# Query turns on quarters of the array, one tile for two kinds of turns, bias copies on a third engine, and a new list of steps

## The chip, the core and the metric

The kernel runs on one core of one Trainium2 chip. The core has five engines with an instruction queue each: TensorE (PE, matrix products, with its weight loads shown as PEld), VectorE (DVE), ScalarE (ACT), GpSimd (POOL) and SyncE (SP), which here only issues DMAs. Each engine works off its own queue in order; semaphores hold an instruction back until what it needs is done. [...] The metric is the device time of one execution in microseconds (us), lower is better.

## What is computed

Eight batches of linear attention (8 heads, 576 positions, head size 64), whose result goes, as 4608 tokens of 512 numbers, through a gated layer with two 512x512 weights:

```python
q_s = exp(q - max(q, -1));  q_s = q_s / sum(q_s, -1)      # over the head's 64 numbers
k_s = exp(k - max(k, 2));   k_s = k_s / sum(k_s, 2)       # over the 576 positions
kv  = einsum('bhsd,bhse->bhde', k_s, v)
x   = einsum('bhsd,bhde->bhse', q_s, kv)                  # then to (b s, h e)
H   = maximum(x @ w_h, 0)
T   = 1 / (1 + exp(-(x @ w_t + b_t)))
out = T * H + (1 - T) * x
```

## The kernel before

**Tiles.** The tokens make 36 tiles of 128. A pair of batches gives nine: four of the first batch, four of the second, and one that is half of each. Tiles 0, 4 and 5 are worked in two halves of the columns, and the last one (35) has its gate in two pieces.

**Order.** All work is written as a list of 683 steps, `ORDER` (line 16), and issued in that order with the scheduler switched off. A step's name gives the function, the batch or tile, and a part; a letter behind a colon gives the engine where there is a choice (A is ACT, D is DVE, P is POOL). Since every engine runs its own queue in order, the list fixes each engine's sequence; between engines the tile framework puts in the semaphore waits, from which tile each instruction writes and reads.

**A batch.** `q`, `k`, `v` (lines 180 to 206) issue the loads on SP's queue, on which the stores `st` stand too. `ek` and `eq` take exponentials on ACT, `vc` casts v (POOL, ACT or DVE). `kv` (262) sums k times v over the positions on PE: for batches from 2 on, 72 products of 64x64 by 65 columns, in which the row half of the array, `hh`, and the column half, `w`, change from one to the next, so that each quarter of the array has one in turn. The two row halves write to two PSUM banks. `kr` and `kn` normalise the result on DVE.

**The turn of q.** `qt` (310) transposes exp(q) of a batch in three groups, the first two (g = 0, 1) with eight products of 128x128 each against an identity, the third with two. It writes a tile `qps` of one PSUM bank from the pool `ps_q`, which holds one such tile. `qc` (329) copies it to SBUF (`eq`) on ACT or DVE.

**A tile.** `xu` (348) multiplies q with kv on PE, `rs` and `x` (367, 372) divide by q's sum on DVE. `xt` (379) transposes x on PE into the first half of a PSUM bank of its own, `turned`, and `xe` (387) copies that to SBUF (`xT`) on DVE or ACT. `bw` (394) puts the bias into the gate's PSUM tile: a product with ones on PE, or, with A, a copy of the prepared rows `ball` on ACT. On top of it `mt` (406) adds four products with w_t, `mh` (414) makes four with w_h. `th` is the tanh on ACT, `dd` joins x and the product with w_h on DVE, `uu` multiplies the two (DVE, or, with P, two instructions on POOL), `oo` adds x on POOL, and `st` stores. `fill` (165) issues products of zeros on PE that nothing reads. Before the first `mh` the weight w_h, in two loads (`w_h_0`, `w_h_2`), has an identity subtracted on POOL (`whd`) and is cast on ACT (`whc`).

The lines that hold the turns' places (100, 101, 115; line 313 in `qt`, 381 in `xt`):

```python
ps_q = pool("ps_q", 1, space=PS)
ps_xt = pool("ps_xt", 1, space=PS)
turned = ps_xt.tile([P, 2, 4, P], FP16, tag="xtps", name="turned")
t = T[f"qps{b}_{g}"] = ps_q.tile([P, a, 4, s * NP], FP16, tag="qps", name=f"qps_{b}_{g}")
t = T[f"xtps{i}"] = turned[:, 0]
```

Of the kernel before, what the change touches and what calls it, by code (L numbers as in the profile page):

```python
# [8 lines left out]
FP32 = mybir.dt.float32  # L9
# [12 lines left out]
wtc_2:P whc_2:A mh_1_0 wtc_0:P vc_1_3 ek_1_3 ek_1_2 vc_1_0 xe_3_0:D mh_3_0 dd_1 xt_0_1 xt_0_0 mt_1_0 xe_0_0:D mh_0_0
xe_0_1 dd_3 xt_2_0 mh_0_1 mt_0_1 th_1_0 xe_2_0:D dd_0 vc_1_2:A kv_1_1 uu_1_0 oo_1_0 eq_1_0 mt_0_0 th_0_0 ek_1_0 ek_1_1
kr_1_1 bw_3 qt_1_0 vc_1_1:A kn_1_1 qc_1_0 mt_3_0 xu_5_1 uu_0_0 mh_2_0 th_3_0 bw_2 rs_5_1 x_5_1 dd_2 xu_4_1 kv_1_0
kr_1_0 eq_1_1 rs_4_1 xt_5_1 mt_2_0 th_2_0 kn_1_0 bw_5 xe_5_1:D x_4_1 xu_5_0 mt_5_1 qt_1_1 eq_1_2 rs_5_0 x_5_0 xt_5_0
xu_4_0 bw_4:A uu_3_0:P oo_3_0 xe_5_0:D mh_5_1 rs_4_0 x_4_0 mh_5_0 xt_4_1 qc_1_1:A xt_4_0 xe_4_1:D dd_5 eq_2_0 xe_4_0:D
v_4_0 mt_5_0 th_5_0 xu_6_0 qt_1_2 rs_6_0 qc_1_2 oo_0_0 mt_4_1 mh_4_1 mh_4_0 uu_2_0:P x_6_0 mt_4_0 eq_2_1 xt_6_0 xu_8_0
uu_5_0 bw_6:A xe_6_0:D qt_2_0 rs_8_0 x_8_0 mh_6_0 oo_5_0 th_4_0 xt_8_0 dd_4 uu_4_0 xu_7_0 mt_6_0 ek_2_0:F rs_7_0
vc_2_2:A bw_8 xe_8_0:D mt_8_0 x_7_0 th_6_0 xt_7_0 th_8_0 oo_2_0 vc_2_0 kv_2_0 oo_4_0 qc_2_0 q_4_0 bw_7:A qt_2_1
qc_2_1:A dd_6 uu_6_0:P oo_6_0 eq_3_0:F xe_7_0:D kr_2_0 kn_2_0 mh_8_0 xu_9_0 rs_9_0 x_9_0 mt_7_0 th_7_0 bw_9 dd_8  # L30
uu_8_0:P qt_2_2 qc_2_2:A xu_10_0 bw_10:A xt_9_0 xe_9_0:D rs_10_0 x_10_0 ek_3_0 mh_7_0 dd_7 ek_3_2 mh_9_0 xu_12_0 k_4_0
xt_10_0 k_5_0 rs_12_0 qt_3_0 xe_10_0:D x_12_0 mt_9_0 th_9_0 uu_7_0:P q_4_9 dd_9 xu_11_0 qc_3_0 vc_3_2:A xt_12_0
mt_10_0 rs_11_0 mh_10_0 x_11_0 v_5_0 q_5_0 vc_3_0 st_1_1 q_5_9 uu_9_0 dd_10 oo_7_0 kv_3_0 qt_3_1 th_10_0 oo_8_0 st_1_0
xe_12_0 bw_12:A mh_12_0 kr_3_0 qc_3_1:A kn_3_0 xu_14_0 rs_14_0 x_14_0 bw_11:A xt_11_0 xe_11_0 mt_12_0 th_12_0 qt_3_2
v_6_0 xt_14_0 oo_9_0 k_6_0 xu_13_0 q_6_0 xe_14_0 mh_11_0 dd_12 qc_3_2 mt_11_0 rs_13_0 eq_4_0:F th_11_0 uu_12_0
uu_10_0:P x_13_0 dd_11 xu_15_0 rs_15_0 vc_4_0 mh_14_0 x_15_0 st_5_1 dd_14 qt_4_0 oo_10_0 vc_4_2 xu_16_0 rs_16_0 x_16_0
xt_13_0 xe_13_0:D oo_12_0 bw_14:A bw_13:A ek_4_0:F st_3_0 mt_14_0 th_14_0 xu_17_0 rs_17_0 bw_15:A x_17_0 qc_4_0
xt_15_0 mt_13_0 kv_4_0 xe_15_0:D kr_4_0 uu_11_0:P oo_11_0 th_13_0 qt_4_1 uu_14_0:P st_3_1 mh_13_0 vc_5_2 xt_16_0
kn_4_0 mh_15_0 xe_16_0:D vc_5_0 xu_18_0 ek_5_0:F dd_13 xt_17_0 qc_4_1:A uu_13_0 xe_17_0:D dd_15 rs_18_0 oo_14_0
bw_16:A mt_15_0 mh_16_0 x_18_0 th_15_0 uu_15_0:P mt_16_0 dd_16 mh_17_0 oo_13_0 bw_17:A th_16_0 oo_15_0 kv_5_0 uu_16_0  # L40
kr_5_0 kn_5_0 oo_16_0 eq_4_2 dd_17 qt_4_2 xt_18_0 eq_5_0 mt_17_0 st_5_0 xe_18_0 xu_20_0 rs_20_0 mh_18_0 qc_4_2:A
bw_18:A q_7_0 th_17_0 mt_18_0 eq_5_1 bw_20:A uu_17_0:P x_20_0 xt_20_0 dd_18 vc_6_2 xe_20_0:D xu_21_0 th_18_0 rs_21_0
st_7_0 v_7_0 qt_5_1 qc_5_1:A mt_20_0 x_21_0 xt_21_0 uu_18_0 eq_5_2 xu_19_0 xe_21_0:D qt_5_0 rs_19_0 x_19_0 st_7_1
mh_20_0 qc_5_0 bw_21:A st_10_1 vc_6_0 mt_21_0 th_20_0 dd_20 ek_6_0:F xu_22_0 bw_19:A rs_22_0 x_22_0 qt_5_2 th_21_0
qc_5_2:A eq_6_0 mh_21_0 bw_22:A xt_19_0 xe_19_0:D kv_6_0 dd_21 kr_6_0 kn_6_0 xt_22_0 uu_20_0:P mh_19_0 mt_19_0
xe_22_0:D dd_19 oo_17_0 xu_23_0 rs_23_0 oo_20_0 oo_18_0 mt_22_0 eq_6_1 qt_6_0 th_19_0 x_23_0 xu_24_0 uu_19_0 th_22_0
# [487 lines left out]
```

## Time and profile before

| | |
|---|---|
| time of three runs | 119.0, 119.03, 119.74 us; median 119.03 |
| span of the profiled execution, first to last instruction | 116.9 us |
| mean granted clock of PE | 0.995 of full |
| bytes moved by DMA | 40.58 MB, 347 GB/s over the span |
| instructions | 3424 |

The span is of one execution taken by the hardware profiler; a run's time also holds what lies before the first and behind the last instruction. The times of the runs are taken without the profiler.

How to read the rows that follow. A row of the timeline has the start in us, the time until the last of the group's instructions ended, the engine, the source line, the operation, the tile written and the tile read, the shape, and how many instructions of the kind stand in a row; a bracket behind it tells how long the engine had been idle and what ended that. PE overlaps its products: one of 128x512 is shown as some 0.38 us long though four of them start within 0.86, so PE's progress is read from start to start. A row of the windows view has the stretch and its length, then for each engine its busy time and its number of instructions, the granted clock, the DMA engines' share and GB/s. A row of the groups view has busy time, mean ns of one, and the idle time before them.

### The profile page before, as it was taken

The numbers are of one execution on the slowest core, as the hardware profiler recorded it, in microseconds if no ns is written. First come the engines' busy times: TensorE is split into PE (matmuls) and PEld (weight loads), VectorE is DVE, ScalarE is ACT, GpSimd is POOL, SyncE is SP. The second block draws the span as 40 slices with busy tenths as digits, with TensorE's granted clock in tenths as the row PEclk, the third lists the DMA queues.
The fourth block names the chain that finished last, engine by engine and source line by source line (L and its number), as shares of the span: only waits on it lengthen the run. The fifth ranks groups of instructions, "written<-read, shape, count | busy, mean of one in ns | idle before, by whom it ended". The sixth has DMA issues, their size and how long they took to land.

```text
span 116.9 us, 3424 instructions
## 1 busy us (share of the span) xinstructions
PE 109.5 (94%) x1351; PEld 61.6 (53%) x1351; DVE 93.3 (80%) x222; ACT 90.0 (77%) x132; POOL 89.1 (76%) x99
## 2 busy tenths in 40 slices
PE   5999987999999999999999999999999999999930
PEld 2354544545665656565665547566564555554520
DVE  5642587589799979979889798988989887899870
ACT  4356461897999999989999999998597998545520
POOL 5022237208996999999999999999989699999960
PEclk9999999999999999999999999999999999999998
DMA  2999999999999999999999999999999956992875
GB/s 42 399 392 377 408 398 385 375 377 379 393 391 397 383 391 393 358 375 387 357 376 360 387 392 363 390 381 383 399 398 217 302 204 270 397 404 115 315 295 179
DMA packets 24195, 40.58 MB, mean 347 GB/s; under 512 B 5362, under 2 KB 11762, under 8 KB 24180
## 3 DMA queue, kind: packets, MB, share of 16 engines
q1 hardware_dynamic: 24032, 40.24, 96.9%
q8 instruction: 10, 0.16, 0.6%
q10 hardware_dynamic: 148, 0.14, 0.4%
q14 instruction: 5, 0.04, 0.1%
HBM read 30.41 MB, written 9.44 MB: 341 GB/s over the span
## 4 chain that ended last, share of the span: by engine, by line
PE 67%; POOL 15%; issue 6%; DVE 5%; DMA 3%; SPq 1%; POOLq 0%; DVEq 0%
PE tps L411 18%; PE gps L419 16%; PE turned L167 9%; POOL o L471 7%; PE xu L361 6%; PE turned L384 5%; PE kv L269 5%; PE qps L324 4%; POOL u L451 4%; DMA out_dram<-o 3%; POOL g L450 2%; PE qps L319 2%; POOL v L259 2%; DVE x L376 2%; PE tps L401 1%
## 5 line engine op out<-in xcount | busy, mean ns | idle before, releaser
L471 POOL TENSOR_TENSOR o<-u,x 128x512 f32<-128x512 f16 (+1 forms) x36 | 40.6, 1143 | 1.6 <-DVE u L453 0.7
L411 PE MATMUL tps<-w16t,xT 128*128 128x512 f16 (+1 forms) x148 | 37.3, 373 | 0.0
L419 PE MATMUL gps<-w16h,xT 128*128 128x512 f16 x144 | 36.8, 379 | 0.5 <-DVE xT L391 0.5
L376 DVE TENSOR_TENSOR x<-xu,rs 128x512 f16<-128x512 f32 (+1 forms) x39 | 25.2, 649 | 2.4
L259 POOL CAST v<-v 128x1152 f16<-128x1152 f32 (+1 forms) x14 | 14.0, 1010 | 14.7 <-DMA v<-in_v_dram 13.7
L439 DVE SCALAR_TENSOR_TENSOR d<-x,gps 128x512 f16<-128x512 f16 x36 | 24.5, 680 | 0.3
L451 POOL TENSOR_TENSOR u<-g,d 128x512 f16<-128x512 f16 x17 | 19.7, 1158 | 1.7 <-DVE rs L370 0.4
L253 ACT ACTIVATE ek<-k 128x576 f16<-128x576 f32 (+2 forms) x15 | 17.9, 1225 | 3.0 <-DMA k<-in_k_dram 3.0
L419 PEld LDWEIGHTS <-xT 128*128 128x128 f16 x144 | 13.0, 98 | 12.3 <-DVE xT L391 1.8
L399 ACT COPY tps<-ball 128x512 f32<-128x512 f32 x28 | 16.6, 597 | 3.5 <-DVE u L453 3.2
L411 PEld LDWEIGHTS <-xT 128*128 128x128 f16 x148 | 13.2, 98 | 10.6 <-DVE xT L391 0.4
L361 PE MATMUL xu<-kvb,eq 128*128 128x130 f16 (+1 forms) x160 | 14.8, 224 | 0.2 <-DVE kvb L287 0.2
L384 PE MATMUL turned<-idh,x 128*128 128x128 f16 x144 | 14.2, 220 | 0.5 <-DVE x L376 0.5
L391 DVE COPY xT<-turned 128x512 f16<-128x512 f16 (+1 forms) x28 | 10.9, 391 | 4.2 <-PE turned L384 3.0
L435 ACT ACTIVATE tps<-tps 128x512 f32<-128x512 f32 (+1 forms) x20 | 11.2, 559 | 3.6 <-PE tps L411 3.3
L453 DVE SCALAR_TENSOR_TENSOR u<-tps,d 128x512 f16<-128x512 f32 (+1 forms) x19 | 12.7, 671 | 1.4 <-ACT tps L435 0.6
L361 PEld LDWEIGHTS <-eq 128*128 128x128 f16 (+1 forms) x160 | 10.0, 100 | 7.3 <-DVE x L376 2.5
L167 PE MATMUL turned<-blank 128*128 128x512 f16 x40 | 12.4, 458 | 1.5 <-POOL blank L149 1.3
L384 PEld LDWEIGHTS <-x 128*128 128x128 f16 x144 | 9.8, 98 | 6.0 <-DVE x L376 2.1
L307 ACT ACTIVATE qe<-q 128x1024 f16<-128x1024 f32 (+3 forms) x9 | 9.4, 1052 | 4.1 <-DMA q<-in_q_dram 4.1
L450 POOL TENSOR_SCALAR g<-th 128x512 f16<-128x512 f16 x17 | 10.6, 621 | 0.9 <-ACT th L433 0.9
L433 ACT ACTIVATE th<-tps 128x512 f16<-128x512 f32 x17 | 10.0, 594 | 0.9 <-PE tps L411 0.9
(48 smaller groups left out, 106.8 us busy)
## 6 DMA issues: line engine op xcount, KB each, us to landing
k<-in_k_dram SPq DMA_DIRECT2D x6, 1152.0 KB, 12.2
v<-in_v_dram SPq DMA_DIRECT2D x6, 1152.0 KB, 12.0
out_dram<-o SPq DMA_DIRECT2D x23, 256.0 KB, 4.0
q<-in_q_dram SPq DMA_DIRECT2D x10, 512.0 KB, 11.5
out_dram<-o SPq DMA_DIRECT2D x6, 512.0 KB, 3.8
k<-in_k_dram SPq DMA_DIRECT2D x4, 576.0 KB, 9.3
q<-in_q_dram SPq DMA_DIRECT2D x2, 1152.0 KB, 14.2
q<-in_q_dram SPq DMA_DIRECT2D x2, 640.0 KB, 10.5
```

Source lines behind the costliest of these rows:

```text
L167: nc.tensor.matmul(spare, blank[:, 0:P], blank, start=True, stop=True, skip_group_check=True)
L253: nc.scalar.activation(t[:, :, c:c + n].rearrange("p j c d -> p c j d"), T[f"k32{b}"][:, c:c + n].rearrange("p c (j d) -> p c j d", j=NJ), ...
L259: copy(v16[b % NV][:, c:c + n, :, 0:D], T[f"v32{b}"][:, c:c + n].rearrange("p c (j d) -> p c j d", j=NJ))
L361: nc.tensor.matmul(dst, turned_q(b, jp, n), kvb[b % NKV][:, hh, kk], start=True, stop=True, skip_group_check=True)
L376: nc.vector.tensor_mul(t[:, k0:k1], sums(i, k)[:, :, :, 0:64], T[f"rs{i}_{k}"][:, 0:k1 - k0].unsqueeze(3).to_broadcast([P, k1 - k0, 4, D]))
L384: nc.tensor.matmul(t[:, n], T[f"x{i}"][:, n0 + n % 2:n0 + 2 * P:2], idh, is_transpose=True, start=True, stop=True, skip_group_check=True)
L399: nc.scalar.copy(t[:, cs], ball[:, cs])
L411: nc.tensor.matmul(T[gate(i, k)][:, cs], T[f"xT{i}"][:, n], w16["t"][:, n, cs], start=False, stop=(n == parts[-1] and not first), skip_gro ...
L419: nc.tensor.matmul(t, T[f"xT{i}"][:, n], w16["h"][:, n], start=(first and n == parts[0]), stop=(n == parts[-1] and not (first and len(part ...
L439: nc.vector.scalar_tensor_tensor(t, T[f"x{i}"], -0.5, T[f"gps{i}"], op0=ALU.mult, op1=ALU.max)
L451: nc.gpsimd.tensor_mul(t, g, T[f"d{i}"])
L471: eng.tensor_add(t[:, cs], T[f"u{i}_{h}"][:, cs], T[f"x{i}"][:, cs])
```

## The change

Six things change.

1. The PSUM pools `ps_q` and `ps_xt`, one bank each, become one pool with one tile of two banks, `turned`, of which all turns of q and of x are slices.
2. For batches 2 to 6 and groups 0 and 1, `qt` issues, in place of eight transposes of 128x128, 32 of 64x64, in which the quarter of the array changes from one to the next; the upper row half writes to the first bank, the lower one to the second. `qc` puts the two together in its copy.
3. `xt` writes to the second bank, tiles of even number to its first half and of odd number to its second.
4. `bw` can copy the bias on DVE. Of 37 bias steps 9 were on PE and 28 on ACT; now 6 are on PE, 22 on ACT and 9 on DVE.
5. The other choices of engine: `uu` on POOL 17 to 20, `vc` on ACT 5 to 8 and on POOL 14 to 11, `xe` on ACT 11 to 16 and on DVE 28 to 23, `qc` on ACT 12 to 8 and on DVE 10 to 14.
6. The whole list is new (679 steps). It has 29 products of zeros instead of 40; the weights load in the order w_h_0, w_t_2, w_t_0, w_h_2 instead of w_h_0, w_h_2, w_t_2, w_t_0; on SP's queue nine stores stand ahead of k_7, as before, and ten instead of seven ahead of v_7.

The code, without the list:

```diff
-    ps_q = pool("ps_q", 1, space=PS)
-    ps_xt = pool("ps_xt", 1, space=PS)
+    ps_ab = pool("ps_ab", 1, space=PS)
...
-    turned = ps_xt.tile([P, 2, 4, P], FP16, tag="xtps", name="turned")
-    spare = turned.rearrange("p a c d -> p (a c d)").bitcast(FP32)
+    turned = ps_ab.tile([P, 2, 2 * DM], FP16, tag="ab", name="turned")
+    spare = turned[:, 1].bitcast(FP32)
...
+    QUADS = (2, 3, 4, 5, 6)
+
+    def corners(b, g):
+        return b in QUADS and g < 2
+
+    def qt_corners(b, g):
+        t = turned[:, :, g * DM:(g + 1) * DM]
+        for n in range(8):
+            for r in range(2):
+                rows = slice(64 * r, 64 * r + 64)
+                for c in range(2):
+                    cols = slice(64 * c, 64 * c + 64)
+                    if b in WIDE:
+                        main = T[f"qe{b}"].rearrange("p j c d -> p (j c d)")[:, 0:MAIN]
+                        main = main.rearrange("p (hh j kk f) -> p j hh kk f", j=4, hh=2, kk=2)
+                        src = main[rows, 2 * g + n // 4, n % 2, n % 4 // 2, cols]
+                        dst = t[cols, r, 64 * n:64 * n + 64]
+                    else:
...
+                    nc.tensor.matmul(dst, src, idh[rows, rows], is_transpose=True, start=True, stop=True,
+                                     skip_group_check=True)
+
     def qt(e, b, g):
+        if corners(b, g):
+            qt_corners(b, g)
+            return
...
-        t = T[f"qps{b}_{g}"] = ps_q.tile([P, a, 4, s * NP], FP16, tag="qps", name=f"qps_{b}_{g}")
+        t = T[f"qps{b}_{g}"] = turned[:, 0, 0:a * 4 * s * NP].rearrange("p (a n t) -> p a n t", a=a, n=4)
...
     def qc(e, b, g):
...
+        if corners(b, g):
+            src = turned[:, :, g * DM:(g + 1) * DM]
+            if b in WIDE:
+                copy(t.rearrange("p a n (r t) -> p r (a n) t", r=2), src.rearrange("p r (m t) -> p r m t", m=8))
+            else:
+                copy(t.rearrange("p a (k r) t -> p r (a k) t", r=2), src.rearrange("p r (m t) -> p r m t", m=4))
...
     def xt(e, i, k):
-        t = T[f"xtps{i}"] = turned[:, 0]
+        t = T[f"xtps{i}"] = turned[:, 1, i % 2 * DM:(i % 2 + 1) * DM].rearrange("p (n t) -> p n t", n=4)
...
     def bw(e, i, h=0):
...
         if e == "A":
             nc.scalar.copy(t[:, cs], ball[:, cs])
+        elif e == "D":
+            nc.vector.tensor_copy(t[:, cs], ball[:, cs])
```

(For the last tile's second gate piece `bw` uses the first bank of `turned` where it used `ps_q`.)

Places of the new list, in its own order, that the prediction speaks of:

```
... kv_1_0 qt_1_1 x_4_1 kr_1_0 kn_1_0 th_2_0 oo_1_0 uu_2_0:P xu_4_0 xt_4_1 rs_4_0 x_4_0 xu_5_0 rs_5_0 qc_1_1:A bw_4
xt_4_0 k_3_0 xu_7_0 oo_2_0 xe_4_1:D mh_4_1 mt_4_1 x_5_0 rs_7_0 th_3_0 eq_1_2 oo_0_0 x_7_0 xe_4_0 mt_4_0 bw_7:D xt_7_0
xe_7_0:D xu_6_0 eq_2_0 eq_2_1 q_3_0 uu_3_0:P qt_1_2 ...
... kv_3_0 qt_3_0 xt_11_0 uu_5_0:P oo_5_0 dd_12 qc_3_0:A bw_9:D mt_9_0 kr_3_0 kn_3_0 xe_11_0:D uu_12_0 qt_3_2 ...
... qt_4_0 uu_13_0:P q_5_9 x_15_0 bw_14:A qt_4_1 qc_4_0 kv_4_0 mh_16_0 dd_14 v_6_0 mt_14_0 eq_4_2 bw_16:A kr_4_0 kn_4_0
xu_18_0 oo_11_0 oo_13_0 qt_4_2 uu_9_0:P dd_16 qc_4_1:A xt_15_0 ...
... xt_20_0 xt_17_0 x_21_0 vc_5_0:A kv_5_0 dd_15 xe_17_0:D oo_14_0 kr_5_0 kn_5_0 dd_18 xe_20_0 qt_5_0 ...
... xt_23_0 oo_18_0 xe_23_0 eq_6_0 qt_5_2 mh_19_0 ...
... kv_6_0 qc_5_2 bw_24:D kr_6_0 q_7_9 qt_6_0 xt_25_0 xe_25_0 kn_6_0 dd_22 qc_6_0:A mt_24_0 xu_26_0 qt_6_1 ...
```

More of the change, by code (lines that the diff above doesn't have):

```diff
@@ L22 @@
[L22 to L46, printed above, removed]
@@ new lines @@
+dd_0 q_2_0 ek_1_2 mh_2_0 mt_2_0 dd_3 bw_3:A ek_1_1 dd_2 qc_1_0:A kv_1_1 mt_3_0 k_2_0 ek_1_0 vc_1_0 v_2_0 uu_0_0:P
+vc_1_1:D eq_1_1 kr_1_1 kn_1_1 xu_4_1 rs_4_1 qt_0_2 qc_0_2 kv_1_0 qt_1_1 x_4_1 kr_1_0 kn_1_0 th_2_0 oo_1_0 uu_2_0:P
+xu_4_0 xt_4_1 rs_4_0 x_4_0 xu_5_0 rs_5_0 qc_1_1:A bw_4 xt_4_0 k_3_0 xu_7_0 oo_2_0 xe_4_1:D mh_4_1 mt_4_1 x_5_0 rs_7_0
+th_3_0 eq_1_2 oo_0_0 x_7_0 xe_4_0 mt_4_0 bw_7:D xt_7_0 xe_7_0:D xu_6_0 eq_2_0 eq_2_1 q_3_0 uu_3_0:P qt_1_2 rs_6_0
+x_6_0 mh_4_0 dd_4 qc_1_2 mt_7_0 th_4_0 qt_2_1 xt_6_0 xe_6_0:D uu_4_0:P xu_8_0 rs_8_0 qc_2_1 ek_2_0:F x_8_0 bw_6:A
@@ new lines @@
+bw_16:A kr_4_0 kn_4_0 xu_18_0 oo_11_0 oo_13_0 qt_4_2 uu_9_0:P dd_16 qc_4_1:A xt_15_0 rs_18_0 qc_4_2 mt_16_0 eq_5_0
+eq_5_1 x_18_0 xu_17_0 xe_15_0:D th_14_0 bw_15:A rs_17_0 xt_18_0 qt_5_1 mt_15_0 oo_9_0 xe_18_0:D th_16_0 x_17_0 xu_20_0
+uu_16_0 oo_16_0 mh_18_0 uu_14_0:P rs_20_0 ek_5_0:F st_10_1 mh_15_0 bw_18:D x_20_0 xu_21_0 qc_5_1 st_10_0 rs_21_0
+mt_18_0 xt_20_0 vc_5_2:A xt_17_0 x_21_0 vc_5_0:A kv_5_0 dd_15 xe_17_0:D oo_14_0 kr_5_0 kn_5_0 dd_18 xe_20_0 qt_5_0
+mh_20_0 xt_21_0 dd_20 th_18_0 bw_17:A mt_17_0 th_15_0 uu_15_0 qc_5_0:A xe_21_0 xu_19_0 uu_18_0:P th_17_0 bw_20:A q_6_0
@@ L394, in bw @@
     def bw(e, i, h=0):
-        bank = (ps_t, "tps") if i < LAST or h == 0 else (ps_q, "qps")
-        t = T[gate(i, h)] = bank[0].tile([P, DM], FP32, tag=bank[1], name=f"tps_{i}_{h}")
+        if i < LAST or h == 0:
+            t = T[gate(i, h)] = ps_t.tile([P, DM], FP32, tag="tps", name=f"tps_{i}_{h}")
+        else:
+            t = T[gate(i, h)] = turned[:, 0].bitcast(FP32)
         cs = columns(i, h)
```

59 lines of the change are left out of this document (39 added, 20 removed).

## The prediction

> **What bounds the kernel now.** First the page's busy table, then the windows of ten microseconds, then PE's timeline and the chain of waits.
>
> ```profile
> PE 109.5 (94%) x1351; PEld 61.6 (53%) x1351; DVE 93.3 (80%) x222; ACT 90.0 (77%) x132; POOL 89.1 (76%) x99
> ```
>
> ```profile
> 60.00:70.00 10.00, 10.00 (x136) 5.44 (x134) 8.62 (x19) 9.34 (x14) 9.79 (x11) 1.00 1.07 378
> ```
>
> The columns after the window's length are busy PE, PEld, DVE, ACT, POOL, then granted clock, DMA share and GB/s. Four engines and the DMA are near full, but PE alone leaves nothing. A busy PE can hide waits, so I look at how closely its starts follow each other:
>
> ```profile
> 61.03 0.39 PE L384 MATMUL turned<-idh,x 128*128 128x128 f16 x4
> 61.25 1.03 PE L419 MATMUL gps<-w16h,xT 128*128 128x512 f16 x4
> 62.11 0.40 PE L361 MATMUL xu<-kvb,eq 128*128 128x130 f16 x4
> 62.35 0.39 PE L384 MATMUL turned<-idh,x 128*128 128x128 f16 x4
> 62.57 1.03 PE L411 MATMUL tps<-w16t,xT 128*128 128x512 f16 x4
> ```
>
> From start to start: four transposes of x (xt) 0.22 us, four products with w_h (mh) 0.86, four xu 0.24, and no hole. The stream runs so from about 20.8 us to its last group:
>
> ```profile
> 111.05 1.04 PE L411 MATMUL tps<-w16t,xT 128*128 128x256 f16 x8
> ```
>
> ```profile
> 113.07 0.41 DVE o L471
> ```
>
> The second line ends the chain of waits; behind it come only the last store and the end of the program. In the last third that chain runs over POOL, which works just behind PE's results. So the end is PE's stream plus a tail of some 5 us: what is added to the stream or put as a hole into it counts in full. The span is 116.9 us, the median of the runs 119.03, so 2.1 us lie outside the span; I add differences to 119.03.
>
> **The quarters.** Ten groups (two of each of batches 2 to 6) lose 8 transposes each and get 32 quarter transposes. No quarter transpose is in this trace; the nearest row is the key-value product kv, also on 64x64 quarters and issued in the same order of quarters.
>
> ```profile
> 9.87 0.48 PE L269 MATMUL kv<-v,ek 64*64 64x65 f16 x36
> 10.28 1.25 PE L167 MATMUL turned<-blank 128*128 128x512 f16 x5
> ...
> 41.98 0.38 PE L401 MATMUL tps<-b,ones 128*128 128x512 f16 x1
> 42.20 0.28 PE L324 MATMUL qps<-idh,qe 128*128 128x128 f16 x2
> ...
> 47.67 1.03 PE L419 MATMUL gps<-w16h,xT 128*128 128x512 f16 x4
> 48.62 0.78 PE L269 MATMUL kv<-v,ek 64*64 64x65 f16 x72
> 49.33 0.62 PE L324 MATMUL qps<-idh,qe 128*128 128x128 f16 x8
> 49.79 1.03 PE L419 MATMUL gps<-w16h,xT 128*128 128x512 f16 x4
> ...
> 57.38 0.42 PE L361 MATMUL xu<-kvb,eq 128*64 128x130 f16 x8
> 57.74 0.40 PE L384 MATMUL turned<-idh,x 128*128 128x128 f16 x4
> ```
>
> 36 products take 0.41 us, 72 take 0.71: 8.3 ns each and 0.11 fixed; and 48.62 is 0.09 later than four products after 47.67 would end, so a block on quarters standing alone pays 0.20. 32 quarters are 0.27 beside a kv and 0.47 alone, against 0.46 for the old eight. In the new list six groups touch a kv (2_0, 3_0, 4_0, 4_1, 5_0, 6_0), four stand alone: 6 x 0.19 saved, 4 x 0.01 lost, **-1.1 us**. The other end is the half-array xu at 57.38, 0.36 us for 8 of 130 columns, 22 ns for 64 columns: 32 of those are 0.71 us, +2.5 in all. I stay with kv, the same tile shape.
> [...]
>
> **Bias.** PE's own bias products (bw) go from nine to six at 0.22 (41.98 to 42.20): **-0.65 us**. DVE gets nine copies. None is in the trace; a bound above is 0.65 each, the DVE row that moves 512 f32 once, below it 0.42, DVE's xT copy of 512 f16:
>
> ```profile
> L376 DVE TENSOR_TENSOR x<-xu,rs 128x512 f16<-128x512 f32 (+1 forms) x39 | 25.2, 649 | 2.4
> ```
>
> ```profile
> 61.45 0.42 DVE L391 COPY xT<-turned 128x512 f16<-128x512 f16 x1 [0.53 <-PE turned L384]
> ```
>
> That is 3.8 to 5.9 us, less five xT copies that go to ACT (2.1) and three u at about 0.65 that go to POOL: DVE comes out 0.3 us below to 1.9 above its 93.3. No path by itself, but its cover gets thinner.
>
> **The start.** Fills fall from 40 to 29. They only fill waits for loads: nothing. But w_h_2 moves from the second to the fourth weight load.
>
> ```profile
> 15.13 0.89 POOL L226 TENSOR_TENSOR w32h<-w32h,idf 128x128 f32<-128x128 f32 x2 [0.38 <-DMA w32h<-in_moe_w_h_dram]
> 19.01 1.04 POOL L222 CAST w16t<-w32t 128x1024 f16<-128x1024 f32 x1 [0.27 <-DMA w32t<-in_moe_w_t_dram]
> ```
>
> ```profile
> 14.78 1.06 ACT L232 ACTIVATE w16h<-w32h 128x1024 f16<-128x1024 f32 x1 [0.90 <-POOL w32h L226]
> ```
>
> ```profile
> 18.14 1.03 PE L419 MATMUL gps<-w16h,xT 128*128 128x512 f16 x4
> 19.67 1.04 PE L419 MATMUL gps<-w16h,xT 128*128 128x512 f16 x4 [0.50 <-DVE xT L391]
> ...
> 20.76 1.03 PE L411 MATMUL tps<-w16t,xT 128*128 128x512 f16 x4
> ```
>
> The fourth load is there at 19.01 (the same eight loads stand ahead); its two subtractions take 0.89, its cast 1.06: PE gets the second half of w_h at about 20.96. Before, eight mh products and the transposes qt_0_2 were done by 20.76; now four mh: 0.86 + 0.11 of work left over, and 0.2 later: **+1.15 us**. If other waits cover it, 0.
>
> **The waits.** Before, x's transposes and q's transposes had tiles of their own. Now both are slices of one tile, `turned`, and in the changed kernel as built the waits go by the whole tile, halves and banks alike: qt_5_2, in the first bank, waits for the copy xe_23 out of the second. So places that the list treats as free are not. Prices of a hand-over:
>
> ```profile
> 30.52 0.29 DVE L391 COPY xT<-turned 128x256 f16<-128x256 f16 x1 [0.38 <-PE turned L384]
> ...
> 19.20 0.41 DVE L391 COPY xT<-turned 128x512 f16<-128x512 f16 x1
> ```
>
> ```profile
> 16.39 0.27 PE L324 MATMUL qps<-idh,qe 128*128 128x128 f16 x2
> ```
>
> ```profile
> 16.70 0.37 ACT L333 COPY eq<-qps 128x256 f16<-128x256 f16 x1 [0.86 <-PE qps L324]
> ...
> 49.99 1.01 ACT L333 COPY eq<-qps 128x1024 f16<-128x1024 f16 x1 [0.33 <-PE qps L324]
> ...
> 84.86 0.59 ACT L391 COPY xT<-turned 128x512 f16<-128x512 f16 x1 [1.45 <-PE turned L384]
> ...
> 99.41 0.60 ACT L391 COPY xT<-turned 128x512 f16<-128x512 f16 x1
> 99.88 0.62 ACT L399 COPY tps<-ball 128x512 f32<-128x512 f32 x1
> ```
>
> With the row at 61.45 above: a reader starts 0.42 after four transposes start (61.03, 61.45), 0.31 after two; an eq copy on ACT is 1.01, an xT copy 0.59 on ACT (the next on ACT starts 0.47 after it) and 0.42 on DVE, 0.29 for half; PE starts 0.06 after a copy ends (19.61, 19.67). In the new list, from PE step to PE step, less PE's own work between:
> xt_4_1, qc_1_1 on ACT, xt_4_0: 0.31+1.01+0.06, less 0.45: 0.93. Then xe_4_1, mh_4_1: 0.66 less 0.35: 0.31. xt_7, xe_7, qt_1_2: 0.90 less 0.46: 0.44. xt_11, qc_3_0 on ACT, xe_11 on DVE, qt_3_2: 1.97 less 1.08: 0.89. qt_4_2, qc_4_1 on ACT, xt_15: 1.38 less 0.11: 1.27. xt_17, xe_17, xe_20 on ACT, qt_5_0: 1.55 less 1.02 (kv_5 between): 0.53. xt_23, xe_23 on ACT, qt_5_2: 1.07 less 0.22: 0.85. xt_25, xe_25 and qc_6_0 on ACT, qt_6_1: 1.96 less 1.32: 0.64.
> PE runs in order, so behind each waiting transpose stand the next mh and mt, and for them th, dd and so POOL. Each stretch is separate, so the holes add: **+5.9 us**, more where ACT or DVE is late anyway. They are also pauses in which those engines catch up, so some of PE's small waits of before go. By the code 148 mt (eight of them of half size), 136 mh, 132 xt, 144 xu, 110 qt, eight blocks of kv and seven bw lie behind 20.76; at the spacings above they are 89.5 us of the 91.1 to the stream's end at 111.9. I take half of these 1.6 off, -0.8; bounds 0 and -1.6.
>
> Sum: -1.1 - 0.65 + 1.15 + 5.9 - 0.8 = +4.5: 123.5. As half of the start's term may be covered by other waits I take **123.0 us**.
>
> **Rivals.** (1) Waits by bank. If only accesses of the same bank excluded each other, the first three holes and qt_5_2 would vanish and qt_3_2 would keep 0.4: 3 us less, 120 us. [...] Against it stand the waits as built. It also holds the case that the holes are half as long. 0.10.
> (2) POOL sets the end, and the change is faster: the chain's last third lies on POOL.
>
> ```profile
> 26.56 0.67 POOL L259 CAST v<-v 128x576 f16<-128x576 f32 x1 [3.86 <-DMA v<-in_v_dram]
> ...
> 70.78 0.62 POOL L450 TENSOR_SCALAR g<-th 128x512 f16<-128x512 f16 x1
> 71.48 1.16 POOL L451 TENSOR_TENSOR u<-g,d 128x512 f16<-128x512 f16 x1
> 72.58 2.24 POOL L259 CAST v<-v 128x1152 f16<-128x1152 f32 x2
> ```
>
> Of its three added pairs of g and u (1.78 each) two, of tiles 0 and 1, come where POOL idled for loads, and three casts of v (1.12 each) leave it for ACT: 1.6 us less in the full stretch, 117.4. (ACT's sum so grows by some 1 us: five xT of 0.59 more too, six bias copies of 0.62 and four small eq of 0.37 less. The cast at 26.56 is POOL's last that waits for a load, so I cost it at nothing that v_7 stands behind ten stores on SP's queue instead of seven; k_7 has nine as before.) It decides if PE were several microseconds ahead of its readers, so that holes cost nothing; the gapless starts speak against it. 0.07.
> (3) Quarters at 22 ns: 3.6 us on top, 126.6. 0.05.
> (4) With fewer fills the clock drops in the start.
>
> ```profile
> 115.00:116.00 1.00, 0.00 (x0) 0.93 0.50 165
> ```
>
> PE stopped at 112 and the clock fell only near 115.9; the new start's longest pause, ahead of 20.96, is some 1.5 us by the loads' times. If it fell, up to 5.6 us (the first 13 fills at half speed) at half clock cost 2.8: 125.8. 0.04.
>
> **Numbers.** Forecast 0.74, its own range 121.0 to 125.3. One per cent, 1.2 us, is what a measurement of this kernel can tell from no change. Faster: rival 2 and a little of 1, 0.08. Same (117.8 to 120.2): most of 1, 0.09. Slower: the rest, 0.83. Range 120.3 to 125.5 leaves out rivals 2 and 3, part of 1 and of 4.
>
> **What would show it.** Right: PE holes of 0.5 to 1.3 us ahead of xt_15, qt_3_2, qt_5_2, qt_6_1 and near tile 4, released by copies of `turned`; quarters near 0.27 us beside kv; first mh of tile 1 whole only at 21 us. Wrong: PE starts as dense as before, or a chain without PE before 85 us.

## The result, and the profile after

The changed kernel takes **130.49 us** (median of five runs, 130.06 to 133.19) against 119.03 before: a ratio of **1.094, 95% interval 1.090 to 1.098**. It is slower, as forecast, but by 11.5 us where 4.0 were forecast, and 5 us above the range. The profiled run took 132.64 us at a lowered clock (a mean of 0.970 of full, against 0.98 in the undisturbed runs that the ratio rests on), so the times in its rows run up to 2 us late.

First the page of the changed kernel, busy time and two rows of the timeline in forty slices:

```profile
PE 110.7 (85%) x1577; PEld 62.0 (47%) x1577; DVE 94.9 (73%) x227; ACT 92.4 (71%) x130; POOL 90.6 (69%) x102
...
PE   5979667998689798979957688997998999999950
...
PEclk9999965899999999999999999999999999999998
```

PE was busy 94% before, now 85%, and every other engine has a smaller share too: the time is in waits, not in work. The timeline's end, PE's last group and DVE's last instruction, shows the same tail of some 5 us as before:

```profile
125.49 0.60 PE L448 MATMUL turned<-w16t,xT 128*128 128x256 f16 x4
```

```profile
127.05 0.42 DVE L508 TENSOR_TENSOR o<-turned,x 128x256 f32<-128x256 f32 x1
```

So the question is what delays PE's stream. The view of PE's waits adds them up by who ended them (total us, times, longest). All of before, 2.7 us:

```profile
PE turned L167 <- POOL blank L149: 1.3, 1, 1.3
PE gps L419 <- DVE xT L391: 0.5, 1, 0.5
PE turned L384 <- DVE x L376: 0.5, 1, 0.5
PE turned L167 <- DVE xT L391: 0.2, 1, 0.2
PE xu L361 <- DVE kvb L287: 0.2, 1, 0.2
```

After, the longest nine of 18 rows, which have 14.7 us in all (417 is `xt`, 349 a whole turn of q, 329 a quarter turn, 361 and 366 `qc`, 424 `xe`, 267 `kv`, 165 a product of zeros, 305 `eq`):

```profile
PE kv L267 <- issue: 2.7, 2, 1.8
PE turned L165 <- POOL blank L147: 1.3, 1, 1.3
PE turned L417 <- DVE eq L366: 1.3, 2, 1.0
PE turned L417 <- ACT eq L361: 1.1, 1, 1.1
PE turned L349 <- DVE xT L424: 1.0, 2, 0.7
PE turned L349 <- ACT qe L305: 0.8, 2, 0.5
PE turned L165 <- DVE eq L366: 0.8, 1, 0.8
PE turned L349 <- ACT xT L424: 0.8, 1, 0.8
PE turned L417 <- ACT eq L366: 0.8, 1, 0.8
```

Most rows are turns that wait for the copy of another turn out of the shared tile. The first is of another kind: `issue` means that PE waited for nothing the profile shows. The eight places that the prediction named are all there; here they are in the timeline, with the idle time in the bracket:

```profile
34.26 0.27 PE L417 MATMUL turned<-idh,x 128*128 128x128 f16 x2 [0.77 <-ACT eq L366]
...
34.99 0.60 PE L456 MATMUL gps<-w16h,xT 128*128 128x512 f16 x2 [0.22 <-DVE xT L424]
...
37.46 0.27 PE L349 MATMUL turned<-idh,qe 128*128 128x128 f16 x2 [0.35 <-DVE xT L424]
...
58.48 0.27 PE L349 MATMUL turned<-idh,qe 128*128 128x128 f16 x2 [0.70 <-DVE xT L424]
...
72.95 0.38 PE L417 MATMUL turned<-idh,x 128*128 128x128 f16 x4 [1.10 <-ACT eq L361]
...
81.82 0.45 PE L329 MATMUL turned<-idh,qe 64*64 64x64 f16 x32 [0.43 <-ACT xT L424]
...
89.70 0.27 PE L349 MATMUL turned<-idh,qe 128*128 128x128 f16 x2 [0.78 <-ACT xT L424]
...
98.96 0.45 PE L329 MATMUL turned<-idh,qe 64*64 64x64 f16 x32 [0.36 <-ACT eq L361]
```

The brackets sum to 4.7 us. A bracket counts from the end that the product before is shown with, which lies behind the moment at which the next could have started (the four transposes of x at 25.36 us are shown 0.39 long, and the next group starts 0.23 after them). From start to start, less the spacing of the product before (as the prediction reckons), the eight are 0.93, 0.39, 0.51, 0.86, 1.26, 0.64, 0.94 and 0.56 us, **6.1** in all, and the two without releaser 3.1.

By the brackets, with the 2.7 without releaser and the 2.7 that the kernel before had as well, 4.6 us of the 14.7 are left: 2.4 more than before in the first 22 us, and 2.2 strewn over the rest (more from start to start, as the part on the prediction works out). From 18 to 24 us the clock was at half speed too, which the prediction had given 0.04: columns as before, the sixth is the granted clock.

```profile
18.00:21.00 3.00, 2.33 (x16) 1.63 (x15) 1.09 (x3) 1.21 (x2) 2.59 (x5) 0.50 1.07 368
21.00:24.00 3.00, 3.00 (x13) 1.38 (x11) 1.16 (x3) 0.71 (x2) 0.08 (x1) 0.50 1.06 392
```

### The profile page after: what moved, and what is told of

Its sections match the earlier page's. It is cut to its first block, busy times and chain, and to the rows that moved or that the text cites. A ratio compares the mean times of both kernels' runs of the same rounds, so it can differ in the third digit from the quotient of the medians.

```text
span 130.9 us, 3893 instructions
## 1 busy us (share of the span) xinstructions
PE 110.7 (85%) x1577; PEld 62.0 (47%) x1577; DVE 94.9 (73%) x227; ACT 92.4 (71%) x130; POOL 90.6 (69%) x102
## 4 chain that ended last, share of the span: by engine, by line
PE 54%; DVE 22%; ACT 8%; issue 7%; DMA 4%; SPq 1%; POOL 0%; DVEq 0%; POOLq 0%
PE gps L456 15%; PE tps L448 14%; PE turned L165 7%; DVE x L409 7%; PE turned L417 5%; DMA out_dram<-o 4%; PE xu L394 4%; PE kv L267 4%; DVE d L476 3%; DVE u L490 2%; DVE xT L424 2%; ACT xT L424 2%; PE turned L329 2%; DVE eq L366 2%; DVE rs L403 2%
## 5 line engine op out<-in xcount | busy, mean ns | idle before, releaser
L488 POOL TENSOR_TENSOR u<-g,d 128x512 f16<-128x512 f16 x20 | 23.1, 1155 | 4.2 <-DVE d L476 1.8
L487 POOL TENSOR_SCALAR g<-th 128x512 f16<-128x512 f16 x20 | 12.3, 617 | 6.2 <-ACT th L470 6.2
L470 ACT ACTIVATE th<-tps 128x512 f16<-128x512 f32 x20 | 11.9, 596 | 6.6 <-PE tps L448 6.5
L434 ACT COPY tps<-ball 128x512 f32<-128x512 f32 x22 | 13.0, 593 | 1.4 <-DVE u L490 1.0
L424 DVE COPY xT<-turned 128x512 f16<-128x512 f16 (+1 forms) x23 | 9.2, 404 | 5.9 <-PE turned L417 3.5
L424 ACT COPY xT<-turned 128x512 f16<-128x512 f16 (+1 forms) x16 | 8.7, 546 | 6.7 <-PE turned L417 4.7
L257 POOL CAST v<-v 128x1152 f16<-128x1152 f32 (+1 forms) x11 | 10.5, 969 | 4.1 <-DMA v<-in_v_dram 4.1
L472 ACT ACTIVATE tps<-tps 128x512 f32<-128x512 f32 (+1 forms) x16 | 9.1, 568 | 5.3 <-PE tps L448 5.2
L403 DVE RECIPROCAL rs<-xu 128x8 f32<-128x8 f32 (+1 forms) x39 | 7.6, 198 | 5.4 <-PE xu L394 5.4
L490 DVE SCALAR_TENSOR_TENSOR u<-tps,d 128x512 f16<-128x512 f32 (+1 forms) x16 | 10.7, 668 | 0.9 <-ACT tps L472 0.4
```

Source lines behind the costliest of these rows:

```text
L424: copy(t[:, 2 * k0:2 * k1], T[f"xtps{i}"][:, 2 * k0:2 * k1])
L434: nc.scalar.copy(t[:, cs], ball[:, cs])
L488: nc.gpsimd.tensor_mul(t, g, T[f"d{i}"])
L490: nc.vector.scalar_tensor_tensor(t[:, cs], T[gate(i, h)][:, cs], 1.0, T[f"d{i}"][:, cs], op0=ALU.add, op1=ALU.mult)
```

## The experiments

The theories, by the numbers that the expectations use: (1) waits of the whole shared tile; (2) PE's instructions do not come fast enough where quarters and kv stand together; (3) the clock drops in the start; (4) the rest is the new list's own; (5) bias copies hold back VectorE. The rival of each is that its cost is hidden by something else. All times are medians; all ratios are to the kernel before, which ran beside each (118.89 to 119.03); a difference given "by the ratios" is that of two ratios, times 119 us.

| run | us | ratio, 95% interval |
|---|---|---|
| changed kernel | 130.49 | 1.094 (1.090 to 1.098) |
| split copies | 131.03 | 1.101 (1.097 to 1.105) |
| two tiles (and split copies) | 127.65 | 1.075 (1.072 to 1.077) |
| whole turns | 128.99 | 1.088 (1.082 to 1.094) |
| more fills | 131.51 | 1.107 (1.103 to 1.111) |
| other weight order | 131.07 | 1.100 (1.097 to 1.103) |
| bias on PE again | 132.54 | 1.114 (1.107 to 1.121) |
| three steps moved | 129.06 | 1.085 (1.077 to 1.093) |
| two tiles, whole turns | 125.05 | 1.052 (1.047 to 1.057) |
| the same, bias on PE again | 126.36 | 1.062 (1.059 to 1.065) |
| two tiles, quarters in three batches | 126.11 | 1.056 (1.051 to 1.062) |
| two tiles, whole turns, other weight order | 124.23 | 1.046 (1.040 to 1.051) |
| the same, four steps moved | 122.23 | 1.026 (1.021 to 1.031) |
| old list in the changed code | 134.73 | 1.132 (1.125 to 1.140) |
| before, one tile | 134.54 | 1.130 (1.125 to 1.135) |
| before, five bias copies on DVE | 121.59 | 1.021 (1.019 to 1.023) |
| before, more products | 126.85 | 1.065 (1.060 to 1.070) |

### The shared tile

Two tiles need the copy of a quarter group as two, so a control has that alone.

```diff
-            src = turned[:, :, g * DM:(g + 1) * DM]
+            for r in range(2):
+                src = turned[:, r, g * DM:(g + 1) * DM]
...
```

> The changed kernel, but the copy qc of each of the ten quarter groups is made as two, one per bank; the control for the run with two tiles. All theories: within 1 us of the changed kernel's 130.5 us (ten more copies; half of the copy of 1024 numbers costs little more than half). If PE's holes are set by how long these copies take, up to 2 us more.

```diff
-    turned = ps_ab.tile([P, 2, 2 * DM], FP16, tag="ab", name="turned")
+    turned = [ps_ab.tile([P, 2 * DM], FP16, tag=f"ab{r}", name=f"turned{r}") for r in range(2)]
```

> As the control with split copies, but the one tile of two banks is two tiles of a bank each, so that waits go by the bank. Theory 1 (the waits of the whole tile make the holes ahead of xt_4_0, mh_4_1, qt_1_2, qt_5_2, partly qt_3_2): 2 to 3 us less than the control, those holes under 0.2 us; the holes ahead of xt_15, qt_5_0, qt_6_1 stay, since quarters and copies lie in both banks. Rival (the holes are made good elsewhere, PE waits for its readers anyway): under 0.7 us less.

The control is 0.5 us over the changed kernel, the two tiles 3.4 under the control (3.1 by the ratios): theory 1, a little over the 2 to 3 that it gave. In PE's waits the copies ahead of xt_4_0, qt_1_2, qt_3_2 and qt_5_2 are gone, and the holes ahead of xt_15 (1.2 us), qt_5_0 (0.4) and qt_6_1 (0.3) have stayed, as expected. As the same turn then waits only for what lies in its bank, this is also what the first rival of the prediction would have been worth, had the waits gone by the bank.

The sharing alone, put into the kernel before:

```diff
-    ps_q = pool("ps_q", 1, space=PS)
-    ps_xt = pool("ps_xt", 1, space=PS)
+    ps_ab = pool("ps_ab", 1, space=PS)
...
+    QUADS = ()
...
+        t = T[f"xtps{i}"] = turned[:, 1, 0:DM].rearrange("p (n t) -> p n t", n=4)
```

> The kernel before with one edit: the turns of q and of x are slices of one tile (q in the first bank, x in the second, no quarters, its own list), so that each waits for the other's copies. Theory 1: clearly slower, by the waits of a list that was not made for it, 5 us or more (124 or more), with PE waiting for copies of the turns. Rival (waits by bank decide on the chip, the tile does not matter): within 0.5 us of 119.

It costs **15.5 us**, more than the whole change. The two longest of PE's waits in it, of 15.0 us in all where the kernel before had 2.7:

```profile
PE turned L418 <- DVE eq L367: 3.3, 3, 1.7
PE turned L418 <- ACT eq L367: 1.9, 4, 1.1
```

No work is added and no two places overlap; `xt` waits for copies of q's turns because they are slices of one tile. The old list with the quarters as well comes out the same (by the code, turns of x here overwrite parts of q's turn before these are copied, so what it computes is not the layer; no instruction is left out, and its time can be read):

> The changed kernel's code (one tile of two banks, quarters) with the list of the kernel before (bias on PE and ACT, its weight order, its fills). Theory 4 (most of what the two causes leave is the new list's own: its start, its order, its engines): below 126 us. Rival (the list was made for the shared places and the old one suffers more under them): 130 us or more.

134.73 us, the rival: the old list suffers more under the shared places than the new one, by 4.2 us. What the new list costs by itself shows only where the sharing is undone (below).

Do the holes count in full? Three steps of the changed kernel moved:

```diff
-... qt_1_2 rs_6_0 x_6_0 mh_4_0 ...
+... rs_6_0 x_6_0 mh_4_0 qt_1_2 ...
-... qt_5_2 mh_19_0 mt_19_0 ...
+... mh_19_0 mt_19_0 qt_5_2 ...
-... kv_4_0 ... qt_4_2 uu_9_0:P dd_16 qc_4_1:A xt_15_0 ...
+... kv_4_0 qc_4_1:A ... qt_4_2 uu_9_0:P dd_16 xt_15_0 ...
```

> The changed kernel with three steps moved in the list: qt_1_2 behind mh_4_0, qt_5_2 behind mt_19_0 (products that are ready hide the copy they wait for), and the copy qc_4_1 from behind qt_4_2 to behind kv_4 (so that xt_15 finds it done). Theory 1 (each hole is its own and counts in full to the end): 0.5 + 0.95 + 1.3 us by PE's starts, 2.3 to 2.8 less, about 127.9. Rival (the pauses let VectorE and ScalarE catch up, and what goes there comes back as another wait): under 1.2 us less.

1.4 us less (1.1 by the ratios, whose intervals overlap), nearer to the rival. The timeline says why. The hole ahead of qt_1_2 went, but the next turn then waited:

```profile
37.63 0.44 PE L329 MATMUL turned<-idh,qe 64*64 64x64 f16 x32 [0.57 <-DVE eq L366]
```

The hole ahead of xt_15 went for good. In the changed kernel ScalarE had stood idle there for 4.91 us, since its copy stood behind qt_4_2 in the list and so waited for that turn to be written to the same tile:

```profile
71.88 1.01 ACT L361 COPY eq<-turned 128x1024 f16<-128x1024 f16 x1 [4.91 <-PE turned L349]
```

### The quarters

```diff
     def qt(e, b, g):
-        if corners(b, g):
-            qt_corners(b, g)
-            return
...
+        if corners(b, g):
+            t = turned[:, :, g * DM:(g + 1) * DM].rearrange("p a (n t) -> p a n t", n=4)
```

> The changed kernel with the quarter turns undone: the ten groups are eight transposes of 128x128 each again, into the same places of the same tile, with the same list. My prediction's term: 1.1 us more than the changed kernel (131.6), since quarters beside kv are cheaper. Theory 2 (the unpaid term: after a dense stretch of quarters and kv PE runs out of instructions, the holes of 0.88 and 1.83 us inside kv_2 and kv_4 without any releaser): those two holes go, so 1.5 to 2 us less than the changed kernel (128.5 to 129). If the holes belong to kv alone they stay.

128.99, 1.5 us less: the quarters cost, where the prediction had them save 1.1. (By the ratios it is 0.7, and the intervals overlap; the same edit on two tiles, below, gains 2.6, clear of them.) Both holes without releaser are gone. In the changed kernel they stand inside kv_2 and kv_4, just behind quarter turns:

```profile
43.38 0.45 PE L329 MATMUL turned<-idh,qe 64*64 64x64 f16 x32
43.65 0.78 PE L267 MATMUL kv<-v,ek 64*64 64x65 f16 x70
45.30 0.22 PE L267 MATMUL kv<-v,ek 64*64 64x65 f16 x2 [0.88 <-issue]
...
66.17 0.70 PE L329 MATMUL turned<-idh,qe 64*64 64x64 f16 x64
66.86 0.64 PE L267 MATMUL kv<-v,ek 64*64 64x65 f16 x55
69.33 0.34 PE L267 MATMUL kv<-v,ek 64*64 64x65 f16 x17 [1.83 <-issue]
```

The kernel with eleven more fills ahead of them (below) has the same two holes, each eleven products earlier in its kv, after 59 instead of 70 and after 44 instead of 55:

```profile
41.88 0.69 PE L268 MATMUL kv<-v,ek 64*64 64x65 f16 x59
43.52 0.31 PE L268 MATMUL kv<-v,ek 64*64 64x65 f16 x13 [0.95 <-issue]
...
65.15 0.54 PE L268 MATMUL kv<-v,ek 64*64 64x65 f16 x44
67.02 0.42 PE L268 MATMUL kv<-v,ek 64*64 64x65 f16 x28 [1.32 <-issue]
```

So the hole belongs to a place in PE's instruction stream, not to a step. Counted in the program (a product and its weight load are two), it is instruction 959 and 1725 in both kernels, 766 apart. With PE's two semaphore instructions between them (at 55.00 and 66.75 us in the changed kernel) they are 768 apart, and of the packets that bring instructions there are three for this stretch (those that start at 49.38, 60.53 and 66.84 us): 256 a packet. The page counts the packets that bring instructions (queue, packets, MB), after and before:

```profile
q8 instruction: 12, 0.20, 0.6%
```

```profile
q8 instruction: 10, 0.16, 0.6%
```

That is 16 KB for some 256 of the 3156 and 2704 instructions. The trace also has the time of each of these packets, beside PE's holes (us; entered is PE's first instruction of the block before):

| hole | block before entered | packet moved | PE goes on |
|---|---|---|---|
| changed kernel, kv_2 | 39.95 | 42.88 to 43.98 | 45.30 |
| changed kernel, kv_4 | 64.70 | 66.84 to 68.07 | 69.33 |
| more fills, kv_2 | 37.62 | 41.00 to 42.05 | 43.52 |
| more fills, kv_4 | 61.10 | 64.52 to 65.72 | 67.02 |

In each, PE goes on 1.3 to 1.5 us after the packet with the next block has landed. Ten of the kernels here have such holes, 19 of 0.2 us and more: all stand at the same place of a block of 256, within one instruction, and all end 1.2 to 1.5 us after a packet. So in these rows the packet with the next block started 2.1 to 3.4 us after PE had entered the block before, and PE was through the two blocks of the changed kernel, with quarter turns and kv in them, at 44.24 and 67.30 us, 1.1 and 2.0 us too soon. The test away from the change is the kernel before with more small products in two places.

```diff
-            for j in range(NJ):
+            for j in ([0] * 16 if b in (3, 5) and kk == 0 else []) + list(range(NJ)):
```

> The kernel before with 64 more products on quarters in kv_3 and 64 in kv_5: the products of the first position block are made 16 times more in the same places, the last of them starting the sum anew, so that the result is the same. Theory 2: row 1983 of PE's instructions (blocks begin at rows 191, 447 and so on) falls near the end of kv_5, and the block before it is nothing but such products: a hole of 2.5 to 5 us without releaser just there, perhaps 1 us at row 1215 in kv_3; with the products' own 1.06 us the time is 122.5 to 126. Rival (instructions are no limit): 120.1, 8.3 ns for each product.

```profile
66.79 1.41 PE L269 MATMUL kv<-v,ek 64*64 64x65 f16 x132
72.41 0.27 PE L269 MATMUL kv<-v,ek 64*64 64x65 f16 x4 [4.21 <-issue]
```

One hole, within four instructions of the place foretold, 4.2 us long; its packet landed at 71.16 us. There is none in kv_3, where the block lasted 5.6 us. At 126.85 us the time is 0.85 over the range expected: of the 7.8 us lost, 1.06 are products and 4.2 the hole, and the rest is put down to the clock, at 0.82 in the ten microseconds behind.

In the changed kernel, does it help to use quarters only where they do not starve?

```diff
+        if b in (3, 5, 6) and g < 2:
+            qt_corners(b, g)
+            return
```

> Two tiles, and the quarters kept for batches 3, 5 and 6 alone; batches 2 and 4, beside whose kv PE ran dry, turn whole. Theory 2 (PE's instructions come in blocks of 256 rows, and a block that PE works off in less than some 5 us makes it wait): the holes without releaser inside kv_2 and kv_4 are gone, at most one of under 1 us at row 1215, and the quarters save their 0.19 us beside kv_3, kv_5 and kv_6: 124.4 to 125.3, at or under the 125.05 of whole turns. Rival (quarters cost by themselves, wherever they stand): 126 to 127.

Not clearly: the two holes went and the one of 0.75 us at instruction 1215 (at 53.52 us) is the one allowed for, but with 125.7 us by its ratio, between the two ranges, the kernel is 0.6 over two tiles with whole turns alone, the intervals overlapping. The quarters showed a saving in no run.

### The bias copies

```diff
-... bw_7:D ... bw_10:D ... bw_9:D ... bw_18:D ...
+... bw_7 ... bw_10 ... bw_9 ... bw_18 ...
```

> The changed kernel with the nine bias copies of VectorE made as products on PE again. My prediction's term (a copy on VectorE is free, a product on PE 0.22 us): 2.0 us more, 132.5. Theory 5 (as in the kernel before with five such copies: each holds VectorE 0.6 us, and x and the copies of x come late for PE): 0.5 to 2.5 us less, 128 to 130.

132.54: 2.05 more for nine, 0.23 each, near the prediction's 0.22. Theory 5 falls. It came from this run of the kernel before:

```diff
-... bw_3 ... bw_2 ... bw_5 ... bw_8 ... bw_9 ...
+... bw_3:D ... bw_2:D ... bw_5:D ... bw_8:D ... bw_9:D ...
```

> The kernel before with five of its nine bias products (tiles 2, 3, 5, 8, 9) made as copies on VectorE and nothing else changed. My prediction's term of 0.22 us for each: 1.1 us less, 117.8. Rival (VectorE is near enough to full that five copies of 0.68 us each come late for PE): no change or up to 1 us more.

There five copies cost 2.6 us instead of saving 1.1. Two of PE's waits, at 31 and 40 us, are new:

```profile
PE tps L413 <- DVE xT L391: 1.5, 2, 0.8
```

```profile
30.12 0.69 DVE L401 COPY tps<-ball 128x512 f32<-128x512 f32 x1
30.85 0.29 DVE L391 COPY xT<-turned 128x256 f16<-128x256 f16 x1
```

The copy of x at 30.85 us, behind a bias copy of 0.69 us on VectorE, comes late. Why the changed kernel is spared this is argued, not tested: the new list gives VectorE five copies of x and three u less, and has the bias copies later. The same on two tiles with whole turns:

> Two tiles, whole turns, and the nine bias copies as products on PE: the new list with none of the change's three costs but the places that lie in both banks. If the bias copies cost what they did in the kernel before (0.5 us each): 121 to 123. If they are free here: 127.

126.36, 1.3 us more with the nine on PE, 0.15 each: nearer to the second, and the copies pay there too.

### The start

```diff
-... whd_0:P kv_0_1 kr_0_1 ... bw_0 kr_0_0 ... xu_0_0 rs_0_0 ... mh_0_0 xu_3_0 ...
+... whd_0:P kv_0_1 fill_3 kr_0_1 ... bw_0 fill_2 kr_0_0 ... xu_0_0 fill_4 rs_0_0 ... mh_0_0 fill_2 xu_3_0 ...
```

> The changed kernel with eleven more products of zeros between 13 and 21 us (after kv_0_1, bw_0, xu_0_0 and mh_0_0). Theory 3 (the granted clock of 0.5 to 0.64 in 17 to 24 us is set off by PE's pauses there, each of about 1 us, and costs 2 to 3.5 us): the clock stays over 0.9 in 18:24 and the time falls by 1.5 to 3 us. My prediction (fills cost nothing and hide nothing): no change, within 0.5 us. If the fills stand in the way of ready work: 1 us more.

The clock stayed up, in the windows view:

```profile
18.00:21.00 3.00, 2.22 (x22) 1.51 (x23) 1.23 (x4) 1.41 (x3) 1.96 (x4) 1.00 1.07 369
21.00:24.00 3.00, 3.00 (x21) 1.51 (x18) 1.83 (x4) 1.16 (x4) 0.51 (x1) 1.00 1.06 393
```

but the time is 131.51, 1 us more. The mean clock of its four runs was 0.991 to 0.999, that of the changed kernel's five 0.969 to 0.982. The split copies, with no fill added, had a clock of 1.00 there in their profile; two of their runs took 130.2 and 130.8 us at 0.998 and 0.996, a third 131.3 at 0.983. So the clock is worth something, some 0.8 us between these, but a full clock does not bring the time under 130, and theory 3 explains little of the 11.5 us. Nor does the trace show the fills in the way of ready work: kv_5 starts at 78.35 us with them and at 78.62 in the split copies. Behind it PE runs out of instructions once more, and qt_5_2 starts at 88.82 instead of 87.73:

```profile
85.30 0.33 PE L418 MATMUL turned<-idh,x 128*128 128x128 f16 x3 [1.21 <-issue]
```

The microsecond is this third hole (its packet landed at 83.88 us): eleven products more had moved the blocks' bounds among the steps.

```diff
-... w_h_0 whd_1:P w_t_2 ... whd_0:P ... bc w_t_0 wtc_0:P w_h_2 whd_2:P whd_3:P ...
+... w_h_0 w_h_2 whd_1:P w_t_0 ... whd_0:P whd_2:P whd_3:P ... bc w_t_2 wtc_0:P ...
```

> The changed kernel with the weights loaded in the order w_h_0, w_h_2, w_t_0, w_t_2 and POOL's subtractions in that order. My prediction's term (w_h_2 as fourth load costs 1.15 us, or nothing if other waits cover it): 0 to 1.15 us less, 129.3 to 130.5. If the start is bound by its waits for copies of x (two before the first product with w_h): within 0.4 us.

131.07, nothing gained: there the copies of the turns hold back the first products anyway. With two tiles and whole turns, both edits of above in one, the weights do show:

> Two tiles of a bank each and no quarter turns, in the new list: both edits of the runs before in one. If the two causes are separate (3.4 us from the waits by bank, 1.5 from the quarters' instructions), they add: about 126.1 us. If the one covers the other: 127 to 127.6. What then stands between it and the 118.9 of the kernel before, some 7 us, is the new list itself and the two-bank hand-overs that are left.

125.05, a microsecond better than additive (3.4 and 1.5 would leave 126.1), and in it PE waits for the second half of w_h:

```profile
21.08 0.59 PE L454 MATMUL gps<-w16h,xT 128*128 128x512 f16 x2 [1.06 <-ACT w16h L230]
```

The same with the weights' edit:

> Two tiles and whole turns (125.05 us), with the weights loaded in the order w_h_0, w_h_2, w_t_0, w_t_2. There PE waits 1.06 us for the cast of w_h's second half. My prediction's term (1.15 us, less what other waits cover): 0.5 to 1.1 us less, 124 to 124.5. If the start is bound by other work of ScalarE anyway: within 0.4 us of 125.05.

124.23: 0.8 us, as expected, though the intervals overlap; that wait is gone.

### What is left

```diff
-... qt_1_2 rs_6_0 x_6_0 mh_4_0 dd_4 qc_1_2 ...
+... qt_1_2 qc_1_2 rs_6_0 x_6_0 mh_4_0 dd_4 ...
-... qt_1_1 x_4_1 kr_1_0 kn_1_0 ...
+... qt_1_1 kr_1_0 kn_1_0 x_4_1 ...
-... kv_4_0 ... qt_4_2 uu_9_0:P dd_16 qc_4_1:A xt_15_0 ...
+... kv_4_0 qc_4_1:A ... qt_4_2 uu_9_0:P dd_16 xt_15_0 ...
```

> Two tiles, whole turns, the weights in the other order, and four steps moved in the list: qc_1_2 right behind qt_1_2, kr_1_0 and kn_1_0 ahead of x_4_1, qc_4_1 behind kv_4. Theory (what is left over the kernel before are waits of the new list, each with its place): the holes of 0.65, 0.27 and 1.16 us ahead of qt_2_1, xu_4_0 and xt_15 go, 1.2 to 2.2 us less than the kernel with the weights alone. Rival (they come back at the next step, as after the first moved list, where half came back): under 0.8 us less.

122.23: 2.0 us less, clear of the intervals, and the three holes are gone. This is what the order of the list costs at three places. 3.2 us over the kernel before are left; they were not taken apart further. No version beat the kernel before.

## Why the prediction was wrong

Its frame held: PE's stream sets the end, the tail is unchanged, holes in the stream move the end. By its own steps:

**The quarters: the step that failed first.** The price of a product was right: 64 quarters take 0.69 us here (66.17 to 66.86), 32 take 0.27. What failed is "I stay with kv, the same tile shape": a kv brings 144 instructions at that pace in the kernel before, with slow ones around, and the fastest block of 256 there lasts 7.1 us (instructions 959 to 1214, 43.7 to 50.8 us). With quarters beside kv PE was through a block in 4.3 and 2.6 us (39.95 to 44.24 and 64.70 to 67.30). What it costs when the next block is not there yet was put at nothing, with no reason given. The term was -1.1; undoing the quarters gains 1.5 us, or 2.6 on two tiles (127.65 to 125.05), and the trace shows 2.7 us of holes for it, 3.1 from start to start. Why the packet did not come sooner was not shown.

**The bias.** -0.65 for three products less: about right, as nine cost 0.15 to 0.23 us each here. That VectorE's cover got thinner was right too, and the kernel before shows the price without cover. VectorE's sum left out the four copies of q's turn that came to it from ScalarE; with 94.9 us against 93.3 it stayed in the range all the same.

**The start.** w_h_2 as fourth load was put at +1.15, or 0 under other waits. In the changed kernel it is 0; where the other waits are gone it is 0.8. But these other waits were missing from the sum: of the waits through the shared tile only those from tile 4 on were counted, while the fills wait 0.8 and the first `xt` 1.0 us for copies of q's turn. The start's waits grew by 2.4 us by the brackets. Eleven fills less, at 0.22 us each, take as much off PE again, so that at a full clock little is left of it (below). "They only fill waits for loads: nothing" held in so far as putting eleven back gained nothing.

**The eight holes.** +5.9 was forecast; from start to start, as it was worked out, the trace has 6.1, all at the named places. The working was right in place and in size. That the holes add was only half right: three were undone by moved steps, worth 2.3 to 2.8, and the end came 1.1 to 1.4 us earlier.

**Before's own waits: the other step that failed.** -0.8 had the wrong sign. It took the new list to be as dense as the old one outside the eight places. The trace has 2.2 us of other waits after the start by the brackets, some 3.8 from start to start by the sum below (for exp(q), for kv's normalised result, for x, for copies of turns, for ScalarE's bias copies). One of them, ahead of xu_4_0, was undone by a moved step; that the list makes the others too is read from what they wait for and was not tested.

**Put together**, for the profiled run, in which PE's last product starts 14.0 us later than before (125.8 against 111.8 us). An estimate from the starts: PE had done the first eight of the 84 us of xu, xt, mh, mt and kv that both kernels have, at the spacings above, by 26.1 us before, by 28.8 in the changed kernel and by 26.9 in the split copies, whose clock was full. So the start costs 2.7 us in this run, 2.0 of them with the clock; without these it is 0.8, where the forecast had 0.65 (1.15 less the half that might be covered). The other 11.3 are -1.1 - 0.65 + 6.1 + 3.1 and 3.8 that are left for the strewn waits. The forecast of 4.0 so missed the holes without releaser (3.1), the strewn waits (3.8 where -0.8 stood) and the clock (2.0 in this run). The strewn waits were not taken apart.

**The rivals.** The third (22 ns a quarter) is refuted by the 0.69 us for 64. The second (POOL) did not decide: POOL has 0% of the chain of waits now, 15% before. The fourth saw the clock drop; it fell after pauses of no more than 1.0 us (0.98 ahead of 17.12 us) and took 2.0 us in the profiled run, within the 2.8 given, but it is a small part of the 11.5, as the split copies show. The first was right in its price of 3 us and wrong in its premise.

## What to carry to other kernels

Before two uses share a tile, list for every access what the tile makes it wait for, over the whole list from the first step: here a tile's name alone cost 15.5 us in one list. Count small products in instructions as well as in nanoseconds: look for 256 instructions of PE that are worked off in less than the 4.0 to 6.9 us that in these runs passed, at the holes, from PE's entry into a block to its first instruction of the next. And when a list of steps is replaced, the waits of the old one say nothing of the new one's: follow each copy to the step that needs it, and check that it does not stand behind a write to the tile it reads.

## What the runs showed of the hardware

PE stood idle for up to 4.21 us with nothing else in its way, at the places where a block of 256 instructions ended. A packet of 16 KB with the next 256 took 0.95 to 1.3 us to move at these holes, and PE went on 1.2 to 1.5 us after it had landed. From PE's entry into one block of 256 to its first instruction of the next, where it had to wait, passed 4.6 us (64.70 to 69.33) and 5.35 (39.95 to 45.30) in the changed kernel, 5.5 in the run with three batches, 5.6 in the one with more products, and 5.9, 5.9 and 6.9 in the one with more fills, whose third hole, 1.21 us inside an `xt`, stands some 512 instructions behind the second; over all 19 holes it was 4.0 to 6.9 us. Blocks that PE took 7.1 us or more for did not make it wait in any of these runs, and some of 5.0 to 5.9 did not either. The entries are read by matching the program's order with the timeline.

The pauses alone did not decide the granted clock here: with pauses of at most 1 us from the first product to 22 us it was 0.50 from 18 to 24 us in the changed kernel's profile and 1.00 in those of the split copies and of the run with more fills. After the pause of 4.21 us, in the run with more products, it was at 0.84 and 0.82 in the stretches of 10 us:

```profile
64.00:74.00 10.00, 5.79 (x158) 3.40 (x156) 4.27 (x11) 4.08 (x8) 7.24 (x7) 0.84 1.06 378
74.00:84.00 10.00, 10.00 (x70) 5.54 (x69) 6.98 (x15) 8.09 (x13) 5.42 (x6) 0.82 1.06 390
```
